# Feed-forward units with a weight scale for each half, and shorter norms at the turn between two layers

## The chip, the cores and the metric

The kernel runs on one core of one Trainium2 chip. The metric is the device time of one execution in microseconds; the median of three runs is compared. Five engines have queues of their own: TensorE (PE; its weight loads are shown as PEld), VectorE (DVE), ScalarE (ACT), GpSimd (POOL) and SyncE (SP), which issues all the DMAs here. They meet in semaphores only.

## What is computed

Three layers in a row, in float32: a retention (attention with a decay mask and no softmax), a mixture of eight experts whose gates are normalised by eight rounds over rows and columns, and a feed-forward layer with a leaky ReLU.

```python
x = retention(q, k, v)                       # 4 x 8 heads x 576 x 64  ->  2304 x 512
# mixture: N, D, E, F = 2304, 512, 8, 1024
for e in range(E):
    out += P[:, e:e+1] * (np.maximum(x @ w1[e], 0.0) @ w2[e])
# feed-forward: 512 -> 2048 -> 512, its weights given in float64
h = x @ w_in
g = np.maximum(0.01 * h, h)
return g @ w_out
```

## The kernel before, in words

**Numbers.** Each float32 operand is scaled by a power of two and split into two float16 parts, high and low; a product is three float16 matmuls. 2 x 2 blocks are multiplied with seven products instead of eight (Winograd's form of Strassen's method), so both operands also need sums of their blocks.

**Units and stages.** The hidden width is worked off in 20 units of 512 columns: 16 of the mixture (two an expert) and 4 of the feed-forward layer (`NU1 = 16`, units 16 to 19). Each unit goes over three thirds of the tokens (`s` = 0 to 2, 384 token pairs each). A stage (unit, s) is 2 x 7 hidden products for the groups g = 0 and 1 (`product_h`, banks hA, hB, hD, hE, line 1028); its second products follow one stage later between the hidden products of the next stage (`group_s`, banks s1a, s1b and s, line 1199). Units 0 and 15 use a plain second product (line 1241). Between both, ScalarE and VectorE split the hidden tiles (hp, hs: lines 1109, 1116, 1119, and sums in lines 1100 to 1146).

**Weights.** `prep_steps(u)` lists the work on a unit's weights as tasks when stage (u - 1, 0) begins. The raw float32 weights come in two halves of 1 MB, part 0 for the first layer and part 1 for the second (`load_raw`, line 186). For each half: four passes of ScalarE that sum magnitudes (`mags`, line 201), a chain of small steps that makes one power of two out of them on all partitions (`scaled`: `total` 207, `quarters` 211 and 213, `beside` 218, `turned` 222 and 223, `spread` 227, `scale` with 159, 160, 165, 250 and 253), four prescaling passes (line 261), and for each group g a `split`: casts on ScalarE (276, 305), differences and block sums on GpSimd (286, 293, 311). In units from 1 on, one chain serves both halves: `scaled(slice(0, 2), maxes(0) + maxes(1))`. The `split` of part 0 asks with `w1_free(g)` that the buffer be free; for g = 1 that is when group 0 of the last stage of the unit before is through. `after(part)` loads the next unit's raw half when a half is split and no operand is on its way to DRAM.

**The order of the work** is written out when the program is built. The class `Order` books each task on engines with estimated costs (`COST`: GpSimd 0.28 us + 0.0020 us an element, and so on) and keeps its own clock `t`. Ahead of and between TensorE's products `tick` calls `pump`, which goes through the queues evac, turn, gate, hid, weights and f64 (hid and weights change places at each call), looks in each at the first 12 tasks (turn: 48) and writes those into their engine's instruction stream whose inputs are done and whose engine is free by the plan within 0.6 us. What isn't out in time is forced: `need((u, "w1", 0))` at the start of stage (u, 0), `need((u, "w2"))` at its first second product. An engine then executes its stream in that order.

**The turn.** While unit 15's second products end, `turn_steps` makes the feed-forward layer's input of each of nine token tiles (two halves h each): sums of magnitudes (lines 1321, 1323), `norms` (a clamp 159, a power of two 160, the factor 1331, the inverse 165), scaling of both halves on GpSimd (1338), four transposes each on TensorE (1348), a copy (64), block sums on GpSimd (532 to 539), casts (64) and low parts (561), and storing to DRAM (486). Stage (16, s) loads what it needs from there (`try_loads`, line 510). `factors` uses the inverses.

Of the kernel before, what the change touches and what calls it, by code (L numbers as in the profile page):

```python
# [8 lines left out]
F32 = mybir.dt.float32  # L9
F16 = mybir.dt.float16  # L10
BF16 = mybir.dt.bfloat16
I32 = mybir.dt.int32
# [3 lines left out]
ALU = mybir.AluOpType  # L16
# [9 lines left out]
NU1 = E * UPE  # L26
# [40 lines left out]
class Order:  # L67


    def __init__(self):  # L70
        self.turn, self.t, self.free = False, 0.0, {e: 0.0 for e in COST}
        self.queues = {q: [] for q in ("evac", "turn", "gate", "hid", "weights", "f64")}

    def book(self, eng, n, after=0.0):
        a, b = COST[eng]
# [20 lines left out]
    def pump(self):  # L96
        self.turn = not self.turn
        qs = list(self.queues.values())
        if self.turn:
            qs[3], qs[4] = qs[4], qs[3]  # L100
        for q in qs:
            for x in q[:WINDOW[q is qs[1]]]:
                if self.ready(x):
                    q.remove(x)
                    self.emit(x)
# [21 lines left out]
def retention_moe_ffn_kernel(ctx: ExitStack, tc: tile.TileContext, qk, vk, wg, wm, wf,  # L127
                             c_dt, c_gq, c_gk, c_id, out):
    nc = tc.nc
    P = 128  # L130
# [39 lines left out]
    wfac = {}  # L170

    raws, raw_at = {}, {}
    turn_last = {}
    order = Order()
    nc_of.update(A=nc.scalar, D=nc.vector, G=nc.gpsimd)

# [11 lines left out]
    def prep_steps(u, small_bank):  # L188
# [16 lines left out]
        def total(p):  # L205
            def f():
                nc.vector.reduce_sum(st["m"][:, p] if u == 0 else m32[:, p], st["mx"][:, p], axis=AX.X)
            return f
# [107 lines left out]
        def add(eng, n, f, deps=(), key=None, cond=None, lat=LAT):  # L316
            x = Task(eng, n, f, deps, (u,) + key, cond, lat)
            tasks.append(x)
            return x
# [6 lines left out]
        def maxes(part, key):  # L326
            there = None if u == 0 else lambda: (u, part) in raws and order.t >= raw_at[u, part] + 8
            return [add("A", 512, mags(part, c), (first_,), key, there) for c in range(4)]

        def scaled(p, mx_, key):  # L330
            t_ = add("D", 10, total(p), mx_, key)
            if u == 0:
                t_ = add("D", 300, top(p), (t_,), key, None, 0.6)
                return add("D", 500, scale(p), (t_,), key, None, 1.2)
            t_ = add("D", 150, quarters, (t_,), key)
            t_ = add("A", 600, beside, (t_,), key)
            t_ = add("D", 150, turned, (t_,), key)
            t_ = add("A", 600, spread, (t_,), key)
            return add("D", 500, scale(p), (t_,), key)

        def scales(part, sc, key):
            return [add("A", 512, prescale(part, c), (sc,), key) for c in range(4)]
# [38 lines left out]
            return tasks  # L381
        ka, kb, k2 = ("w1", 0), ("w1", 1), ("w2",)
        first_ = add(None, 0, begin, (), ka)
        sc = scaled(slice(0, 2), maxes(0, ka) + maxes(1, ka), ka)
        pre0 = scales(0, sc, ka)
        last0 = split(0, 0, pre0[0:2], ka, w1_free(0))
        last0 += split(0, 1, pre0[2:4], kb, w1_free(1))
        after(0, last0, kb)
        pre1 = scales(1, sc, k2)
        last1 = split(1, 0, pre1[0:2], k2, w2_free) + split(1, 1, pre1[2:4], k2, w2_free)  # L390
        after(1, last1, k2)
        return tasks
# [918 lines left out]
    def turn_steps(s, j0):  # L1311

        xs, st = {}, {}

        def sums(j, h):
            def f(e):
                if h == 0:
                    st["l", j] = small.tile([P, 2], F32, tag="l1", name=f"tl1{j}")
                i, o = y[h * NJ + j], st["l", j][:, h:h + 1]
                if e is nc.scalar:  # L1320
                    nc.scalar.activation(junk, i, AF.Abs, accum_out=o)
                else:
                    nc.vector.tensor_reduce(o, i, axis=AX.X, op=ALU.add, apply_absolute_value=True)
            return f

        def norms(j):
            def f():
                s1 = small.tile([P, 2], F32, tag="ts1", name=f"ts1{j}")
                s2 = st["s", j] = small.tile([P, 2], F32, tag="s2", name=f"ts2{j}")
                pow2(s1, st["l", j], f"t{j}")  # L1330
                nc.vector.tensor_scalar(s2, s1, XS, None, op0=ALU.mult)
                recip2(inv.rearrange("p (h j) -> p h j", h=2)[:, :, j], s1)
            return f

        def scaled(j, h):
            def f():
                i = h * NJ + j
                nc.gpsimd.tensor_scalar(y[i], y[i], st["s", j][:, h:h + 1], None, op0=ALU.mult)  # L1338
            return f

        xt = [None, None]

        def turned(j, h):
            def f(e):
                i = h * NJ + j
                ptv = idle_bank(f"xt{i}").rearrange("p (k i) -> p k i", k=NP)
                for k in range(NP):
                    nc.tensor.transpose(ptv[:, k, :], y[i][:, 128 * k:128 * k + 128], ident)
                xt[h] = wtmp.tile([P, NP, P], F32, tag="r64", name=f"tx{i}", bufs=R64)
                copy_on(e, xt[h], ptv)  # L1350
            return f

        j, p, key = j0, turn_last, (1, s)

        def add(eng, n, f, deps, lat=LAT):
            x = Task(eng, n, f, tuple(d for d in deps if d), key, None, lat)
            order.queues["turn"].append(x)
            return x

        y_done = Task(None, 0, None, done=max(order.free["D"], order.free["A"]))  # L1360
        a = [add("AD", 512, sums(j, h), (y_done,)) for h in range(2)]
        a = add("D", 300, norms(j), a)
        b = [add("G", 512, scaled(j, h), (a,)) for h in range(2)]
        t = [add("AD", 512, turned(j, h), (b[h],) + p.get(f"x{h}", ()), 1.5) for h in range(2)]
        operand_tasks(1, j, xt, tuple(t), key, p)
# [11 lines left out]
        try_loads()  # L1377

    def need(key):
        order.flush("weights", lambda k: k == key)  # L1380
        order.wait(max([x.done for x in w_all if x.key == key and x.done], default=None))

# [49 lines left out]
    for n, (u, s) in enumerate(stages):  # L1432
        if s == 0:
            need((u, "w1", 0))
            if u + 1 < NU:
                w_all[:] = w_all[-120:] + prep_steps(u + 1, idle_bank)
                order.queues["weights"] += [x for x in w_all if x.key[0] == u + 1]
            if u == NU1 - 1:
                order.flush("f64", lambda k: True)
        for g in range(2):  # L1440
            if s == 0 and (g == 1 or u == 0):
                need((u, "w1", 1))
            if g == 1 and u == 0:
                logits(s)
                if s == NS - 1:
                    last = ()
                    for f in gate_steps():
                        last = (Task("D", 1500, f, last, "gate", None, 5.0),)
                        order.queues["gate"] += last
            for r in H_ORDER:  # L1450
                need_x(u, s, PROD[r][0])
                product_h(u, s, g, r)
                hpos[0] += 1
                if g == 1:
                    held[0] -= 1
                    try_loads()
                seconds(seconds_by(hpos[0]))
# [70 lines left out]
```

## Time and profile before

| what | us |
| --- | --- |
| median of 3 runs (1801.22 to 1801.67) | 1801.61 |
| the profiled execution | 1801.79 |
| its span | 1799.9 |
| TensorE busy in the span | 1765.2 |
| VectorE busy | 1489.9 |
| ScalarE busy | 1285.3 |
| GpSimd busy | 815.8 |

All rows below are of the profiled execution. A row of a timeline has the start in us from the span's start, the length of a run of equal instructions, engine, line of the kernel, operation, the tile written and the tiles read (buffer and unit numbers left out), shapes, count, and in brackets how long the engine had stood still before it and who released it. Matmuls overlap, so the length of a group is a little more than its step to the next group.

### The profile page before, as it was taken

Reading aid. Unit: us, or ns where it says so; the run is one execution under the profiler, and the core shown is the slowest. Engines: PE = TensorE matmul, PEld = TensorE weight load, DVE = VectorE, ACT = ScalarE, POOL = GpSimd, SP = SyncE. Lnnn points to the kernel's source line nnn. Section 1 sums busy time; section 2 is a strip of 40 time slices with the busy share of each in tenths; the row PEclk is TensorE's granted clock in tenths of the full one; section 3 lists DMA queues with packets and bytes.
Section 4 is the critical chain, followed back from the end, with each engine's and each line's share of the span. In section 5 each row is a group of like instructions: output and inputs, shape, how many; then the busy total and the mean of one; then the engine's idle time right before and its main releaser. Section 6 shows DMA issues by size and latency. Waiting matters only on the chain.

```text
span 1799.9 us, 35885 instructions
## 1 busy us (share of the span) xinstructions
PE 1765.2 (98%) x13686; PEld 1290.1 (72%) x13686; DVE 1489.9 (83%) x2642; ACT 1285.3 (71%) x2808; POOL 815.8 (45%) x782
## 2 busy tenths in 40 slices
PE   9999999999999999999999999999999988999998
PEld 8855677777777777777777777777776555777776
DVE  7955898999888888888898888887776895788886
ACT  6777777777777777777777777777675666877653
POOL 4815362726344463626263444636224972443600
PEclk9999999999999999999999999999999999999999
DMA  9773545446354454454464454443443454444242
GB/s 345 271 252 103 152 127 170 136 150 187 115 171 138 156 156 152 127 170 151 135 190 120 163 147 156 147 143 102 140 150 103 158 170 129 131 125 141 78 128 83
DMA packets 206784, 272.98 MB, mean 152 GB/s; under 512 B 13698, under 2 KB 177556, under 8 KB 201492
## 3 DMA queue, kind: packets, MB, share of 16 engines
q1 hardware_dynamic: 206612, 270.70, 47.9%
q8 instruction: 107, 1.75, 0.4%
q14 instruction: 65, 0.53, 0.1%
HBM read 241.02 MB, written 29.63 MB: 150 GB/s over the span
## 4 chain that ended last, share of the span: by engine, by line
PE 88%; DVE 7%; POOL 2%; issue 1%; ACT 1%; DMA 1%; SPq 0%; DVEq 0%; POOLq 0%; ACTq 0%
PE s L1199 17%; PE hA L1028 12%; PE hB L1028 12%; PE hE L1028 12%; PE s1a L1199 11%; PE s1b L1199 11%; PE hD L1028 6%; PE s L1241 2%; PE s1a L1241 1%; PE s1b L1241 1%; DVE y L1212 1%; DVE xst L561 1%; POOL y L1338 1%; DVE hs L1119 0%; PE xo L721 0%
## 5 line engine op out<-in xcount | busy, mean ns | idle before, releaser
L1028 PEld LDWEIGHTS <-w 128*128 128x128 f16 x5040 | 492.5, 98 | 265.7 <-DMA xring<-x 3.9
L1199 PEld LDWEIGHTS <-hs 128*128 128x128 f16 x3888 | 380.9, 98 | 87.7 <-DVE hs L1119 4.7
L1199 PEld LDWEIGHTS <-hp 128*128 128x128 f16 x2916 | 285.6, 98 | 80.9 <-issue 2.9
L286 POOL TENSOR_TENSOR w<-raw,w 128x384 f16<-128x384 f32 x152 | 163.3, 1088 | 364.1 <-ACT w L276 363.8
L293 POOL TENSOR_TENSOR raw<-raw 128x256 f32<-128x256 f32 x304 | 280.4, 922 | 20.0
L1212 DVE SCALAR_TENSOR_TENSOR y<-s,fac,y 128x256 f32<-128x256 f32 (+1 forms) x322 | 197.6, 614 | 101.2 <-PE s L1199 84.1
L1028 PE MATMUL hE<-xring,w 128*128 128x384 f16 x1440 | 274.7, 326 | 5.3 <-DMA xring<-x 2.1
L1028 PE MATMUL hA<-xring,w 128*128 128x384 f16 x1440 | 276.5, 328 | 2.8 <-ACT w L276 2.3
L1028 PE MATMUL hB<-xring,w 128*128 128x384 f16 x1440 | 274.0, 326 | 0.0
L1199 PE MATMUL s<-w,hs 128*128 128x256 f16 x1932 | 264.2, 273 | 0.8 <-ACT s L1217 0.7
L1119 DVE TENSOR_TENSOR hs<-fs,hs 128x768 f16<-128x768 f32 (+1 forms) x228 | 241.4, 1062 | 8.3 <-ACT hs L1109 6.8
L311 POOL TENSOR_TENSOR w<-raw,w 128x512 f16<-128x512 f32 x148 | 200.4, 1368 | 76.5 <-ACT w L305 76.2
L1109 ACT ACTIVATE hs<-fs 128x768 f16<-128x768 f32 (+1 forms) x228 | 187.6, 823 | 44.4 <-DVE fs L1144 35.1
L446 POOL TENSOR_TENSOR f<-f,e 128x256 f32<-128x256 f32 x64 | 52.8, 825 | 352.5 <-DVE e L438 296.2
L1109 ACT ACTIVATE hp<-fp 128x384 f16<-128x384 f32 x240 | 160.4, 677 | 13.3 <-DVE fp L1067 12.5
L1212 DVE SCALAR_TENSOR_TENSOR y<-s1a,fac,y 128x256 f32<-128x256 f32 (+1 forms) x161 | 98.7, 613 | 50.9 <-ACT s L1217 28.7
L1199 PE MATMUL s1a<-w,hs 128*128 128x256 f16 x972 | 133.4, 273 | 4.6 <-ACT hs L1109 2.4
L1028 PE MATMUL hD<-xring,w 128*128 128x384 f16 x720 | 136.6, 326 | 1.1 <-ACT hD L1056 1.1
L1212 DVE SCALAR_TENSOR_TENSOR y<-s1b,fac,y 128x256 f32<-128x256 f32 (+1 forms) x161 | 98.7, 613 | 43.3 <-ACT s L1217 18.6
L1199 PE MATMUL s1b<-w,hs 128*128 128x256 f16 x960 | 132.1, 273 | 1.8 <-DVE hs L1119 1.4
L1199 PE MATMUL s1a<-w,hp 128*128 128x256 f16 x972 | 132.6, 273 | 1.1 <-DVE y L1212 1.0
L1199 PE MATMUL s1b<-w,hp 128*128 128x256 f16 x960 | 131.6, 274 | 0.5 <-DVE y L1212 0.5
(215 smaller groups left out, 2699.4 us busy)
## 6 DMA issues: line engine op xcount, KB each, us to landing
xring<-x SPq DMA_DIRECT2D x413, 384.0 KB
raw<-in_wm SPq DMA_DIRECT2D x32, 1024.0 KB
r<-in_wf SPq DMA_DIRECT2D x64, 256.0 KB
qk<-in_qk SPq DMA_DIRECT2D x16, 512.0 KB
vk<-in_vk SPq DMA_DIRECT2D x16, 512.0 KB
wf_s<-f SPq DMA_DIRECT2D x32, 256.0 KB
raw<-wf_s SPq DMA_DIRECT2D x8, 1024.0 KB
x<-xst SPq DMA_DIRECT2D x30, 256.0 KB
```

Of the source, the lines that this page charges most:

```text
L286: nc.gpsimd.tensor_tensor(v[0], v[1], v[2], op=ALU.subtract)
L293: nc.gpsimd.tensor_tensor(o, x, y_, op=ALU.subtract)
L311: (nc.gpsimd if u or part else nc.vector).tensor_tensor(lo, r, hi, op=ALU.subtract)
L446: nc.gpsimd.tensor_tensor(dst, dst, cur["tx"].bitcast(F32), op=ALU.mult)
L561: nc.vector.tensor_tensor(st[d][:, :, 1], src[d](), st[d][:, :, 0], op=ALU.subtract)
L1028: nc.tensor.matmul(bank, w[:, a, wi, k, :], x[:, :, b, k, :], start=r in (1, 5) and k == q == 0, stop=k == 1 and q == 2, skip_group_check= ...
L1109: nc.scalar.activation(hid[k][:, 0, a:b], src[:, a:b], AF.Relu if moe and relu else AF.Copy)
L1119: nc.vector.tensor_tensor(t[:, 1, a:b], src[:, a:b], t[:, 0, a:b], op=ALU.subtract)
L1199: nc.tensor.matmul(out_, t[:, a, i, ts], w[:, b, wi, 0, :], start=start and k == 0, stop=k == 5, skip_group_check=True)
L1212: nc.vector.scalar_tensor_tensor(out_, bank, f, out_, op0=ALU.mult, op1=ALU.add)
L1241: nc.tensor.matmul(bank, t[:, a, i, ts], w[:, b], start=l == g == q == 0, stop=l == g == 1 and q == 2, skip_group_check=True)
L1338: nc.gpsimd.tensor_scalar(y[i], y[i], st["s", j][:, h:h + 1], None, op0=ALU.mult)
```

## The change

In units 16 to 19 a half's scale is found from that half alone: part 0 gets its chain after its own four magnitude passes, and part 1's passes and chain are listed behind the splits of part 0. Units 1 to 15 keep one chain for both halves. The six tasks of every such chain go into a queue of their own, which `pump` looks at right behind evac and ahead of the turn, and `need` forces it too. In the turn, the clamp goes (a bound from above on the factor takes its place in the same instruction), the factors of three tiles share one tile, and the inverses of three tiles are computed in one instruction after the third.

```diff
-        self.queues = {q: [] for q in ("evac", "turn", "gate", "hid", "weights", "f64")}
+        self.queues = {q: [] for q in ("evac", "scale", "turn", "gate", "hid", "weights", "f64")}
...
-            for x in q[:WINDOW[q is qs[1]]]:
+            for x in q[:WINDOW[q is qs[2]]]:
...
         def scaled(p, mx_, key):
             t_ = add("D", 10, total(p), mx_, key)
+            first = len(tasks) - 1
...
-            return add("D", 500, scale(p), (t_,), key)
+            t_ = add("D", 500, scale(p), (t_,), key)
+            order.queues["scale"] += tasks[first:]
+            return t_
...
-        sc = scaled(slice(0, 2), maxes(0, ka) + maxes(1, ka), ka)
-        pre0 = scales(0, sc, ka)
+        if u < NU1:
+            sc = [scaled(slice(0, 2), maxes(0, ka) + maxes(1, ka), ka)] * 2
+        else:
+            sc = [scaled(slice(0, 1), maxes(0, ka), ka)]
+        pre0 = scales(0, sc[0], ka)
         last0 = split(0, 0, pre0[0:2], ka, w1_free(0))
         last0 += split(0, 1, pre0[2:4], kb, w1_free(1))
         after(0, last0, kb)
-        pre1 = scales(1, sc, k2)
+        if u >= NU1:
+            sc += [scaled(slice(1, 2), maxes(1, k2), k2)]
+        pre1 = scales(1, sc[1], k2)
...
                 s1 = small.tile([P, 2], F32, tag="ts1", name=f"ts1{j}")
-                s2 = st["s", j] = small.tile([P, 2], F32, tag="s2", name=f"ts2{j}")
-                pow2(s1, st["l", j], f"t{j}")
-                nc.vector.tensor_scalar(s2, s1, XS, None, op0=ALU.mult)
-                recip2(inv.rearrange("p (h j) -> p h j", h=2)[:, :, j], s1)
-            return f
+                s2 = st["s", j] = turn_s[s][:, j - NT_S * s]
+                nc.vector.tensor_scalar(s1.bitcast(I32), st["l", j].bitcast(I32), EXPM, EXPM,
+                                        op0=ALU.bitwise_xor, op1=ALU.bitwise_and)
+                nc.vector.tensor_scalar(s2, s1, XS, XS * 2.0 ** 90, op0=ALU.mult, op1=ALU.min)
+            return f
+
+        def inverses():
+            nc.vector.tensor_scalar(inv_of(s).bitcast(I32), turn_s[s].rearrange("p j h -> p h j").bitcast(I32), -1.0,
+                                    float((254 << 23) + (12 << 23)), op0=ALU.mult, op1=ALU.add)
...
+        if j == NT_S * s + NT_S - 1:
+            order.queues["gate"].append(Task("D", 20, inverses, (a,), "inv"))
...
     def need(key):
+        order.flush("scale", lambda k: k == key)
         order.flush("weights", lambda k: k == key)
```

## Rows read from the trace of the kernel before

**Rows 1.** Busy time by stretches (us; count): PE, PEld, DVE, ACT, POOL; clock; DMA.

```profile
200.00:1350.00 1150.00, 1148.77 (x8777) 858.61 (x8776) 992.68 (x1782) 850.83 (x1859) 514.76 (x497) 1.00 0.48 147
1350.00:1600.00 250.00, 233.77 (x1543) 152.37 (x1542) 189.20 (x327) 176.21 (x387) 135.60 (x125) 0.98 0.42 134
```

**Rows 2.** The same view, finer: the turn, and the stretches of lower clock.

```profile
1410.00:1470.00 60.00, 53.36 (x301) 29.35 (x299) 55.47 (x91) 37.61 (x78) 57.65 (x50) 1.00 0.60 198
...
1470.00:1480.00 10.00, 9.55 (x64) 7.09 (x65) 8.70 (x15) 7.18 (x17) 3.85 (x5) 0.84 0.19 69
...
1510.00:1520.00 10.00, 7.23 (x48) 4.56 (x46) 4.35 (x8) 5.49 (x12) 2.77 (x4) 0.88 0.52 153
1520.00:1530.00 10.00, 6.88 (x37) 3.97 (x36) 4.27 (x4) 5.57 (x12) 8.43 (x10) 0.78 0.00 0
```

**Rows 3.** Timeline of PE where unit 17 begins, and in calm.

```profile
1513.96 0.82 PE L1199 MATMUL s1a<-w,hs 128*128 128x256 f16 x6
1517.05 0.50 PE L1028 MATMUL hA<-xring,w 128*128 128x384 f16 x2 [2.28 <-ACT w L276]
...
1527.93 1.14 PE L1028 MATMUL hB<-xring,w 128*128 128x384 f16 x6
...
1537.63 0.28 PE L1199 MATMUL s1a<-w,hs 128*128 128x256 f16 x1 [0.74 <-DVE hs L1119]
...
1565.50 0.38 PE L1199 MATMUL s1b<-w,hs 128*128 128x256 f16 x2 [0.39 <-POOL w L311]
...
1580.06 0.82 PE L1199 MATMUL s1a<-w,hs 128*128 128x256 f16 x6
...
1584.63 1.14 PE L1028 MATMUL hB<-xring,w 128*128 128x384 f16 x6
```

**Rows 4.** Timeline of ACT, steps of unit 17's weights.

```profile
1446.94 0.63 ACT L201 ACTIVATE junk<-raw 128x512 uint8<-128x512 f32 x1
...
1483.20 0.63 ACT L201 ACTIVATE junk<-raw 128x512 uint8<-128x512 f32 x1
...
1496.47 0.78 ACT L227 COPY m<-t 32x2 f32<-32x2 f32 x4
...
1515.88 0.72 ACT L261 ACTIVATE raw<-raw,sw 128x512 f32<-128x512 f32 x1
```

**Rows 5.** Timeline of POOL: the turn's last tile, then unit 17's first-layer weights.

```profile
1464.37 2.17 POOL L1338 TENSOR_SCALAR y<-y,ts 128x512 f32<-128x512 f32 x1 [0.20 <-DVE inv L165]
...
1476.53 0.77 POOL L532 TENSOR_TENSOR sa<-tx 128x256 f32<-128x256 f32 x1 [6.07 <-DVE tx L64]
...
1517.07 1.78 POOL L286 TENSOR_TENSOR w<-raw,w 128x384 f16<-128x384 f32 x2 [36.77 <-ACT w L276]
1518.93 3.13 POOL L293 TENSOR_TENSOR raw<-raw 128x256 f32<-128x256 f32 x4
1522.78 2.27 POOL L311 TENSOR_TENSOR w<-raw,w 128x512 f16<-128x512 f32 x2 [0.73 <-ACT w L305]
```

**Rows 6.** Timelines of ACT, POOL and PE: unit 16's second half.

```profile
1398.70 0.50 ACT L276 CAST w<-raw 128x384 f16<-128x384 f32 x1
...
1400.19 0.73 ACT L261 ACTIVATE raw<-raw,sw 128x512 f32<-128x512 f32 x1
...
1460.32 2.30 POOL L311 TENSOR_TENSOR w<-raw,w 128x512 f16<-128x512 f32 x2
...
1468.58 0.39 PE L1199 MATMUL s1a<-w,hs 128*128 128x256 f16 x2 [2.15 <-ACT hs L1109]
1470.45 0.40 PE L1199 MATMUL s1a<-w,hs 128*128 128x256 f16 x1 [1.48 <-DVE hs L1119]
```

**Rows 7.** DVE by line: count, ns min/median/max, first and last start in us.

```profile
L159 DVE TENSOR_SCALAR pww<-m x19: 157/162/170, 145.1 to 1654.8; 128x2 f32<-128x2 f32 x19
L159 DVE TENSOR_SCALAR pwt<-tl x9: 155/687/741, 1373.8 to 1462.7; 128x2 f32<-128x2 f32 x9
...
L165 DVE TENSOR_SCALAR inv<-ts x9: 154/159/165, 1374.3 to 1464.1; 128x2 int32<-128x2 int32 x9
```

More of the change, by code (lines that the diff above doesn't have):

```diff
@@ L99, in pump @@
         if self.turn:
-            qs[3], qs[4] = qs[4], qs[3]
+            qs[4], qs[5] = qs[5], qs[4]
         for q in qs:
-            for x in q[:WINDOW[q is qs[1]]]:
+            for x in q[:WINDOW[q is qs[2]]]:
                 if self.ready(x):
@@ L172, in retention_moe_ffn_kernel @@
     raws, raw_at = {}, {}
-    turn_last = {}
+    turn_last, turn_s = {}, {}
     order = Order()
@@ L1358, in add @@
             return x
+        if j == NT_S * s:
+            turn_s[s] = small.tile([P, NT_S, 2], F32, tag="s2", name=f"ts2{s}", bufs=2)
         y_done = Task(None, 0, None, done=max(order.free["D"], order.free["A"]))
@@ L1436, in retention_moe_ffn_kernel @@
                 w_all[:] = w_all[-120:] + prep_steps(u + 1, idle_bank)
-                order.queues["weights"] += [x for x in w_all if x.key[0] == u + 1]
+                order.queues["weights"] += [x for x in w_all if x.key[0] == u + 1 and x not in order.queues["scale"]]
             if u == NU1 - 1:
```

## The prediction

> **What bounds the kernel now.** I read the busy times by stretches first. From 200 to 1350 us TensorE is busy 1148.77 of 1150 us at a granted clock of 1.00; from 1350 to 1600 us it is busy 233.77 of 250 us, at 0.98 [rows 1]. So TensorE bounds the kernel, and an edit on another engine only pays where TensorE stands still or runs at the lower clock. That second stretch is the turn from the first layer to the second: unit 15 ends, its output is normalised, transposed and split into operands, and units 16 and 17 start.
>
> Finer windows [rows 2] show two kinds of trouble in it. From 1410 to 1470 us GpSimd is busy 57.65 and VectorE 55.47 of 60 us: the turn itself. From 1510 to 1530 us TensorE is busy only 7.23 and 6.88 of 10 us with clocks of 0.88 and 0.78, although the turn is over. TensorE's timeline names the reason [rows 3]: at 1517.05 us the first product of unit 17 waits 2.28 us for the first-layer weights of ScalarE's line 276, and the next lines wait on the same tile. The clock falls with the idling.
>
> Why are these weights late? ScalarE's and GpSimd's timelines tell [rows 4, 5]. The sums of magnitudes of unit 17's first half were done by 1447.5 us (the last begins at 1446.94). Those of the second half, whose load waits until unit 16's second layer is split, ended at 1483.7. One scale chain serves both halves, so it starts only then, and crawls behind the hidden tiles: its last four copies begin at 1496.47, the last prescaling pass at 1515.88, when the order written by the planner is out of time and forces it. GpSimd had been idle for 36.77 us when it got its first piece.
>
> **Part 1: own-half scale in units 16 to 19.** Unit 17's chain can start at 1447.5 instead of 1483.7 us. With 68 us until 1515 the four prescalings, four casts and eight GpSimd steps of the first half fit: GpSimd's share is 1.78 + 3.13 + 2.27 = 7.18 us [rows 5]. What the wait cost: from the start of the last group before it (1513.96) to the start of hB (1527.93) is 13.97 us; the same six groups in calm take 1584.63 - 1580.06 = 4.57 us [rows 3]. So 9.40 us, idling and lower clock together, go. A wait of 0.74 us for hidden tiles at 1537.63 [rows 3] comes of it, since VectorE had nothing to do meanwhile; it goes too: **10.14 us**.
>
> Cost: a chain per half instead of one for both adds 8 VectorE steps (a sum, two transposes, two maxima, then three of the scale itself) and 8 ScalarE copies a unit. In units 18 and 19 TensorE has no wait in which these would show, so I set them at nothing; their cover is the slack of the weights, and without it they would cost four times the 2 to 3 us at which part 3 prices such a chain.
>
> One thing moves later. The weights queue looks only at its first 12 tasks. The second group of a first half has exactly 12 (two casts, two differences, four sums, two casts, two differences) and waits until the unit before has finished with its buffer. Before, the second half's magnitude passes stood ahead of these twelve; now they stand behind. In unit 16 one sees the order of before when that gate opened: the cast at 1398.70 and at once the second half's prescaling at 1400.19 [rows 6]. After, at this place four magnitude passes come, then a whole chain, then prescaling. The second-layer weights of unit 16 ended at 1460.32 + 2.30 us before, and TensorE stood until 1470.45 anyway, for hidden tiles (2.15 and 1.48 us) [rows 6]. So a delay of up to 7.8 us is covered by that. I take the delay as 5: the passes take the slots of the prescalings, and GpSimd, full until 1470, started the second layer later than ScalarE offered it.
>
> **Part 2: scale steps served first.** For units 1 to 15 this moves 11 small VectorE steps a unit ahead of the hidden tiles' work. TensorE loses 1.23 us in 1150 there [rows 1], so nothing is to be gained; between -1 and +2 us for a changed order, taken as 0. For units 16 and 17 it is what makes the chain short: 13.3 us from the last magnitude pass to the last copies [rows 4] should become 5 to 9, an estimate from six steps of 0.2 to 0.8 us with a slot of the order between each two.
>
> **Part 3: the norms.** Of four VectorE steps a tile two go (lines 159 and 165), nine times; three joint inversions come instead. In the turn line 159 takes 0.687 us at the median, line 165 0.159 [rows 7]: 0.85 us a tile. Of the six tiles normalised between 1410 and 1470 us that is 5.1 us less of VectorE, in the stretch where it is nearly full. Against it stand the chains that now run in this stretch, unit 16's second half and unit 17's first: 19 steps, at 0.16 to 0.17 us each [rows 7] 3.2 us.
>
> Line 159 says that more is to be counted. With GpSimd idle (the weights' scale, all 19 of them) it takes 0.157 to 0.170 us; in the turn the same form takes up to 0.741 [rows 7]. So two steps of each moved chain that fall beside GpSimd's work can cost 0.53 us more, half of them as I take it: 1.1 us, and the chains 4.3. Net 0.8 us less of VectorE, which I count as 0.8 us of time; bounds are -5.2 (below) and +5.
>
> The Trainium skill (SBUF — State Buffer, section Who interferes with whom) has a rule for this: a VectorE tensor_scalar that uses both ports and a GpSimd instruction exclude each other, whichever issues first holds the ports for its whole length. The trace agrees for line 159, 0.155 against 0.741 us. The rule speaks against the change: it would make most of the moved chains' tensor_scalar steps wait for one GpSimd instruction each. By it the net of part 3 would be near zero or a loss of 1 us.
>
> **The sum.** The profiled execution took 1801.79 us (span 1799.9 and 1.9 around it), 0.2 us above the median of the three runs. 1801.79 - 9.40 - 0.74 - 0.8 = **1790.9 us**. What is late next: in unit 17 its second-layer weights, whose passes start when unit 16's last stage frees the first-layer buffer, near 1500 us. Before, their first use waited 0.39 us for line 311 at 1565.50 [rows 3], so the need comes near 1555; some 38 us of passes, chain and splitting (7.2 of the first half's second group, 17 of its own) leave about 15.
>
> **Rivals.**
> First: the turn's own waits go too. VectorE is behind TensorE's stand at 1468 to 1470 us; 2.15 + 1.48 us of idling and the clock of 0.84 in the ten microseconds after it (1.6 us) make 5.2 us [rows 2, 6]: **1785.7 us**. For it speaks that VectorE is the fuller engine there; against it that GpSimd is as full and the moved chains take most of it back. 0.16.
> Second: unit 17's first half lands in the turn. Its 7.18 us of GpSimd work become ready near 1460, beside tiles 7 and 8. GpSimd has one gap there, the 6.07 us before 1476.53 [rows 5]; what doesn't fall into it, one to three steps of 0.9 to 1.1 us ahead of tile 8's scaling, delays unit 16's third stage, and TensorE pays it with the lower clock on top: 2 to 6 us, **1795 us**. For it: the planner counts 0.28 + 0.002 x 512 = 1.3 us for a scaling that took 2.17 [rows 5], and so sees GpSimd free too early. 0.22, of which 0.03 end within 0.2%.
> Third, slower: unit 16's second half. If the moved chain is as slow in the full turn as unit 17's was, 13.3 us, then with four passes prescaling starts some 20 us late, and the last weights come at 1480 to 1483 in place of 1462.6. TensorE stands 12 us longer, with the lower clock 16: **1807 us**. It decides from a finish near 1478 on, where the loss equals the gain. Against it: the chain is now served ahead of all but evacuations. 0.08.
> Fourth, it doesn't do what it says: unit 17's pieces stay behind the hidden tiles' work, and are forced at 1515 as before: **1801 us**. Against it: 68 us for 16 steps. 0.07.
>
> **How the numbers follow.** The forecast, 1788 to 1794, has 0.47. The range of 1785.0 to 1798.0 takes in most of the first two rivals and leaves out the other two: about 0.8. A run of this kernel can be told from no change by about 0.2%, 3.6 us. Faster: 0.47 + 0.16 + 0.19 = 0.82; the same 0.03 + 0.07 = 0.10; slower 0.08.
>
> **What would show it.** Right: the last prescaling of unit 17's first half begins before 1480 us; no wait of hA on line 276 near 1505; granted clock 1.00 from 1490 to 1530; raw weights of unit 18 loaded 20 us earlier. The norm shows as two short steps a tile. Wrong: s1a waiting on GpSimd's line 311 near 1465 to 1480 (third rival), hA or hE waiting on xring near 1486 (second), or lines 276 and 305 releasing TensorE near 1515 as now (fourth). The order is a plan with its own clock; a stall in the calm stretch, which has none to speak of, would upset the sum too.

## The result and the profile after

The changed kernel takes 1813.51 us (1813.03 to 1817.1, 6 runs), the kernel before 1801.62 us (1800.53 to 1802.86, 6 runs) beside it: 1.007 times as long, 95% interval 1.0057 to 1.0083. It is slower. The profiled execution took 1813.27 us, with a span of 1811.5 us.

Busy time of the changed kernel by stretches, columns as in [rows 1] and [rows 2]:

```profile
200.00:1350.00 1150.00, 1148.15 (x8770) 857.88 (x8768) 1002.24 (x1787) 854.55 (x1864) 510.02 (x498) 1.00 0.48 147
1350.00:1600.00 250.00, 226.28 (x1482) 147.00 (x1481) 180.98 (x311) 168.33 (x374) 132.80 (x120) 0.97 0.43 133
...
1410.00:1470.00 60.00, 54.04 (x306) 30.18 (x304) 53.73 (x96) 42.44 (x96) 55.43 (x50) 1.00 0.58 192
1470.00:1480.00 10.00, 7.00 (x31) 3.80 (x31) 7.27 (x13) 5.78 (x11) 3.06 (x2) 0.66 0.26 96
1510.00:1520.00 10.00, 10.00 (x77) 7.39 (x76) 6.05 (x10) 8.52 (x19) 5.43 (x6) 1.00 0.72 195
1520.00:1530.00 10.00, 10.00 (x79) 7.53 (x78) 5.59 (x9) 8.24 (x21) 2.96 (x2) 1.00 0.44 116
1560.00:1570.00 10.00, 2.35 (x18) 1.56 (x17) 6.70 (x7) 2.71 (x5) 8.52 (x8) 0.83 0.00 0
1570.00:1580.00 10.00, 7.88 (x42) 4.91 (x42) 3.11 (x6) 6.50 (x16) 2.83 (x3) 0.65 0.40 123
```

From 1510 to 1530 us TensorE is now busy throughout at full clock, where [rows 2] had 7.23 and 6.88 us of ten. A hole that was not there stands at 1560 to 1580 us, and the one at 1470 to 1480 us is deeper (7.00 us at 0.66, against 9.55 at 0.84). TensorE's timeline names the releasers; the first two lines answer the last two of [rows 6], those at 1520.56 and 1521.22 us the first two of [rows 3]:

```profile
1471.17 0.61 PE L1207 MATMUL s1a<-w,hs 128*128 128x256 f16 x2 [2.60 <-ACT hs L1117]
1473.05 0.39 PE L1207 MATMUL s1a<-w,hs 128*128 128x256 f16 x1 [1.27 <-DVE hs L1127]
...
1492.87 1.14 PE L1036 MATMUL hA<-xring,w 128*128 128x384 f16 x6 [1.87 <-DMA xring<-x]
...
1520.56 0.82 PE L1207 MATMUL s1a<-w,hs 128*128 128x256 f16 x6
1521.22 1.14 PE L1036 MATMUL hA<-xring,w 128*128 128x384 f16 x6
...
1534.67 0.28 PE L1207 MATMUL s1a<-w,hs 128*128 128x256 f16 x1 [0.60 <-DVE hs L1127]
...
1560.88 0.49 PE L1207 MATMUL s1b<-w,hp 128*128 128x256 f16 x3
1562.76 0.27 PE L1207 MATMUL s1b<-w,hp 128*128 128x256 f16 x1 [1.39 <-ACT w L276]
1565.86 0.38 PE L1207 MATMUL s1b<-w,hp 128*128 128x256 f16 x2 [2.83 <-POOL w L286]
...
1571.26 0.37 PE L1207 MATMUL s1b<-w,hs 128*128 128x256 f16 x1 [4.69 <-ACT w L305]
1572.49 0.59 PE L1207 MATMUL s1b<-w,hs 128*128 128x256 f16 x2 [0.86 <-POOL w L311]
```

Unit 17's first product (1521.22) no longer waits. Its second-layer weights, with 0.39 us of waiting before [rows 3], now hold TensorE for 1.39 + 2.83 + 4.69 + 0.86 = 9.77 us.

To see where time comes and goes, I take the same matmul (the fifth of the six of hD, once in each group) in two timelines and subtract. This table holds its start in the kernel before and the offset of each other kernel, from one profiled execution of each (us; the runs e1 to e16 follow below):

```
product      u16 st1  u16 st2  u16 st3  u17 st1  u17 st2  u17 st2  u19 st3
             group 1  group 1  group 1  group 0  group 0  group 1  group 0
before       1453.31  1484.55  1512.98  1538.40  1566.36  1579.08  1758.69
changed         0.72     4.65     6.60    -2.96     7.79     9.15    11.60
e1_ahead        1.75     4.54     6.75    -1.95    -1.95    -1.95    -1.69
e2_norms       -0.16     0.21     0.16     0.11     0.10     0.10    -0.03
e3_queue        1.01     2.22     3.79     3.07     3.06     3.06     2.57
e4_own          0.10     5.86    14.50    15.27    31.00    31.71    36.50
e10_window     -0.15    -0.81    11.24     1.77     6.35     8.37     8.37
e8_hold         1.38     3.62     3.18    -3.44    10.34    11.95    12.20
e9_nosums       0.89     3.85     5.02    -3.68    -3.68    -3.68    -3.40
e11_both        0.81     2.82     2.14    -4.48     9.29    10.91    11.17
e12_chain       0.97     2.62     4.23    -2.08     5.87     7.55     7.81
e14_slack       0.22    -0.05    -0.53     0.33     0.07     0.07     1.37
e5_ahead17      1.47     3.54     5.76    -2.94    -2.94    -2.94    -2.70
e13_q16         0.35     3.03     5.24    -3.46    -3.46    -3.46    -3.21
e15_q16a17      0.49     3.14     5.36    -3.34    -3.34    -3.34    -3.07
e16_nonorm     -0.69     1.81     4.03    -4.67    -4.67    -4.67    -4.41
```

Where the texts written before the runs speak of the offset of unit 16's third stage or of unit 17's start, they mean where that stage begins: the second and the third column.

The changed kernel gains 6.60 + 2.96 = **9.56 us** at unit 17's start, the predicted 9.40. Against it stand 6.60 - 0.72 = **5.9 us** lost in the turn (third column less the first), 9.15 + 2.96 = **12.1 us** lost at unit 17's second layer, and 11.60 - 9.15 = 2.5 us at the same place in unit 18. (The first column, and the 1 to 2 us that some kernels lose or gain before it, arise mostly in the first 120 us and at one wait near 316 us. e15 and e16, whose work is the same up to the turn, differ by 1.2 us in it, so one offset of that size says little; differences along a row say more.)

ScalarE's and GpSimd's timelines show unit 17's weights, first half then second:

```profile
1447.63 0.63 ACT L201 ACTIVATE junk<-raw 128x512 uint8<-128x512 f32 x1
...
1457.20 0.79 ACT L227 COPY m<-t 32x2 f32<-32x2 f32 x4
...
1484.57 0.71 ACT L261 ACTIVATE raw<-raw,sw 128x512 f32<-128x512 f32 x1
...
1512.33 0.62 ACT L201 ACTIVATE junk<-raw 128x512 uint8<-128x512 f32 x1
...
1529.98 0.62 ACT L201 ACTIVATE junk<-raw 128x512 uint8<-128x512 f32 x1
...
1538.89 0.78 ACT L227 COPY m<-t 32x2 f32<-32x2 f32 x4
...
1546.81 0.72 ACT L261 ACTIVATE raw<-raw,sw 128x512 f32<-128x512 f32 x1
```

```profile
1463.57 2.27 POOL L311 TENSOR_TENSOR w<-raw,w 128x512 f16<-128x512 f32 x2
...
1489.44 4.13 POOL L293 TENSOR_TENSOR raw<-raw 128x256 f32<-128x256 f32 x4
...
1506.63 1.42 POOL L311 TENSOR_TENSOR w<-raw,w 128x512 f16<-128x512 f32 x1 [1.88 <-ACT w L305]
...
1548.98 2.50 POOL L286 TENSOR_TENSOR w<-raw,w 128x384 f16<-128x384 f32 x2 [21.43 <-ACT w L276]
...
1571.29 2.27 POOL L311 TENSOR_TENSOR w<-raw,w 128x512 f16<-128x512 f32 x2 [0.73 <-ACT w L305]
```

The first half's chain starts after 1447.63 us and the weights of its first group are whole at 1508 us, well before 1521. The second half's passes, at 1478.8 to 1483.2 us before [rows 4], run from 1512.33 to 1529.98 us; its last weights end at 1573.56 us, 12.7 us after TensorE comes to the products that want them (1560.88). Before, they ended at 1567.28 us: they are 6.3 us later now and TensorE is there 3.0 us sooner, which is about the 9.4 us of added waiting; with the lower clock behind it, 12.1 us are lost. The same picture as [rows 5], one layer on: GpSimd stands 21.43 us, then gets everything at once. The first line of GpSimd is unit 16's second layer: it ends at 1465.84 us, 3.2 later than before [rows 6].

### The profile page after: what moved, and what is told of

Read it like the earlier page. It is cut to its first block, busy times and chain, and to the rows that moved or that the text cites. A ratio compares the mean times of both kernels' runs of the same rounds, so it can differ in the third digit from the quotient of the medians.

```text
span 1811.5 us, 35925 instructions
## 1 busy us (share of the span) xinstructions
PE 1766.5 (98%) x13686; PEld 1290.8 (71%) x13686; DVE 1496.5 (83%) x2657; ACT 1295.1 (71%) x2840; POOL 811.1 (45%) x782
## 3 DMA queue, kind: packets, MB, share of 16 engines
q8 instruction: 107, 1.75, 0.4%
## 4 chain that ended last, share of the span: by engine, by line
PE 85%; DVE 7%; POOL 4%; DMA 2%; issue 1%; ACT 1%; SPq 0%; DVEq 0%; ACTq 0%; POOLq 0%
PE s L1207 17%; PE hA L1036 12%; PE hB L1036 12%; PE hE L1036 12%; PE s1a L1207 11%; PE s1b L1207 11%; PE hD L1036 6%; PE s L1249 2%; PE s1a L1249 1%; PE s1b L1249 1%; POOL raw L293 1%; DVE y L1220 1%; DVE w L705 1%; POOL y L1350 1%; DVE xt L834 1%
## 5 line engine op out<-in xcount | busy, mean ns | idle before, releaser
L1127 DVE TENSOR_TENSOR hs<-fs,hs 128x768 f16<-128x768 f32 (+1 forms) x228 | 237.3, 1046 | 12.7 <-ACT hs L1117 11.7
L311 POOL TENSOR_TENSOR w<-raw,w 128x512 f16<-128x512 f32 x148 | 193.4, 1321 | 104.1 <-ACT w L305 103.8
```

The source lines that it names most:

```text
L311: (nc.gpsimd if u or part else nc.vector).tensor_tensor(lo, r, hi, op=ALU.subtract)
L1127: nc.vector.tensor_tensor(t[:, 1, a:b], src[:, a:b], t[:, 0, a:b], op=ALU.subtract)
```

## The experiments

Theory A, formed from these rows: the loss is the second half's late passes, and its cure is their place in the list. The rival: the parts themselves (queue, norms, own halves) cost the time.

**e1_ahead**, the changed kernel with the second half's passes listed first:

```diff
         last0 = split(0, 0, pre0[0:2], ka, w1_free(0))
+        if u >= NU1:
+            sc += [scaled(slice(1, 2), maxes(1, k2), k2)]
         last0 += split(0, 1, pre0[2:4], kb, w1_free(1))
         after(0, last0, kb)
-        if u >= NU1:
-            sc += [scaled(slice(1, 2), maxes(1, k2), k2)]
         pre1 = scales(1, sc[1], k2)
```

> The changed kernel, with the magnitude passes and the chain of the second half listed ahead of the second group of the first half, as they stood before. Theory A (the twelve tasks of that group, which wait for their buffer, hide the second half from the queue's window, so its weights come too late): the waits for second-layer weights near 1561 to 1573 us (9.8 us of idling and the lower clock behind it, some 12 us) and near 1655 (2.7 us) go, the gain at the start of unit 17 stays: 1799 +- 3 us; 1794 if the turn's loss of 5 us has the same cause in unit 16. Theory B (ScalarE is too full in unit 16's stages, wherever the passes stand): the second layer stays late, 1808 us or more.

Measured 1799.82 us, ratio 0.9986 (0.9976 to 0.9995). Its waits:

```profile
1472.79 0.61 PE L1207 MATMUL s1a<-w,hs 128*128 128x256 f16 x2 [4.15 <-ACT hs L1117]
1473.78 0.40 PE L1207 MATMUL s1a<-w,hs 128*128 128x256 f16 x1 [0.38 <-DVE hs L1127]
...
1496.70 1.14 PE L1036 MATMUL hB<-xring,w 128*128 128x384 f16 x6 [1.47 <-ACT hB L1046]
...
1563.54 0.38 PE L1207 MATMUL s1b<-w,hs 128*128 128x256 f16 x2 [0.40 <-POOL w L311]
```

The 12.1 and 2.5 us are gone: the second layer waits 0.40 us. The passes end by 1513.1 us and the chain's last copies begin at 1518.37, 20 us sooner. What remains is the turn: 6.75 - 1.75 = 5.0 us. The two waits for hs last 4.53 us together where they lasted 3.63 before [rows 6], only 0.9 us more; but the granted clock behind them is 0.66 instead of 0.84:

```profile
1470.00:1480.00 10.00, 6.83 (x30) 4.31 (x31) 7.26 (x12) 4.84 (x9) 2.32 (x2) 0.66 0.33 125
```

**e2_norms, e3_queue, e4_own**, the kernel before with one part of the change each: the turn's norms, the scale queue, the own halves.

```diff
 e2  norms(j), inverses(), turn_s as in the change
 e3  queue "scale" as in the change
 e4  if u < NU1 / if u >= NU1 in prep_steps as in the change
```

> The kernel before with the shorter norms alone. Theory A (the norms help the turn a little, and its loss of 5 us in the changed kernel comes from the moved weights): 1797 to 1801 us, the waits near 1517 us as before. Theory C (the shorter norms cost the turn its 5 us, by the shared factor tile or by another order of VectorE and GpSimd): 1806 us.

Measured 1803.31 us, ratio 1.0001 (0.9992 to 1.0011): the norms are worth nothing, and cost nothing in the turn (offset 0.16 at unit 17's start).

> The kernel before with the queue for the scale steps alone; the scale still waits for both halves. Theory A: unit 17's chain shrinks from 17 us to some 8, its prescaling begins near 1493 us and not 1503, and most of the 9.4 us at 1517 go, nothing moves into the turn: 1792 to 1796 us. Theory D (serving the chain ahead of the turn's and the hidden tiles' work costs them more than it gives): 1802 us or more.

Measured 1803.46 us, ratio 1.0003 (0.9993 to 1.0013). The queue alone shortens the chain from 13.3 to 11.2 us only (1485.43 to 1496.64) and does not bring unit 17's first layer in time: its passes are still at 1481 to 1485 us, its prescaling at 1503, and the gain at unit 17's start is 3.79 - 3.07 = 0.7 us. With it 2.8 us are lost in the turn (1.01 to 3.79). In the third stage TensorE waits 1.93 us for hs at 1503.28, where it waited 0.60 us before. The 1.2 us of the second stage come without more waiting: hs is waited for 2.17 and 1.49 us as before, but the granted clock from 1470 to 1480 us is 0.66 instead of 0.84. Why it stays low for longer there is not shown.

> The kernel before with the own-half scale alone; chains are served in the weights queue. Theory A: unit 17's first layer is in time, its second layer as late as in the changed kernel or later, because the chain is slower: 1813 to 1820 us. Theory D (the queue is what costs): 1800 us or less.

Measured 1839.44 us, ratio 1.0205 (1.019 to 1.022).

```profile
1474.01 0.37 PE L1204 MATMUL s1a<-w,hs 128*128 128x256 f16 x1 [6.81 <-ACT w L305]
...
1474.04 2.27 POOL L311 TENSOR_TENSOR w<-raw,w 128x512 f16<-128x512 f32 x2 [4.39 <-ACT w L305]
```

Without the queue, unit 16's own second half is late: its weights end at 1476.3 us. That is the prediction's third rival, and the queue is what keeps it away from unit 16. The time is 19 us above the upper end of Theory A, which names unit 17 alone. The offset grows by 14.4 us in unit 16, with a wait of 7.48 us for xring at 1499.68 that follows, and by 16 more in unit 17.

**e10_window**, the changed kernel with the look-ahead of 24 tasks instead of 12:

```diff
-LAT, SLACK, WINDOW = 0.15, 0.6, (12, 48)
+LAT, SLACK, WINDOW = 0.15, 0.6, (24, 48)
```

> The changed kernel with the look-ahead of all queues but the turn's widened from 12 to 24 tasks, nothing else. Theory A, the twelve waiting tasks of a first half's second group hide the second half's passes: the passes of unit 17's second half begin well before 1512 us (1475 to 1495), the wait of 9.8 us at 1562 to 1573 us goes, time 1797 to 1803 us. Theory B, the order of the list delays them in another way: the waits stay, 1811 to 1815 us. As the window is that of the hidden tiles' queue too, some us of change elsewhere are possible.

Measured 1810.08 us, ratio 1.0043 (1.0029 to 1.0057).

```profile
1495.40 2.08 PE L1036 MATMUL hA<-xring,w 128*128 128x384 f16 x6 [9.86 <-DMA xring<-x]
...
1566.11 6.00 POOL L311 TENSOR_TENSOR w<-raw,w 128x512 f16<-128x512 f32 x4
...
1571.05 0.58 PE L1207 MATMUL s1b<-w,hs 128*128 128x256 f16 x2 [3.24 <-POOL w L311]
```

The time lies between the two theories. The loss at the second layer halves (8.37 - 1.77 = 6.6 us), but mostly because TensorE comes there 4.7 us later (1.77 against -2.96): the last weights end at 1572.11 us, 1.5 us sooner than in the changed kernel. Only the first of the four passes moves, to 1470.35 us; the others still come at 1511 to 1530, among the second group's casts. And the wider view reorders the turn itself: TensorE waits 9.86 us for xring. So the window of 12 is at most a small part of the cause. What decides is the order of the list, which e1 changes by itself. In e1, too, three of the four passes begin only at 1510.23 to 1512.47 us, but they stand together; in the changed kernel, with the second group's pieces ahead of them, three begin at 1525.60 to 1529.98. What holds them back there, task by task, is not shown.

**e8_hold**, e1 with the prescaling of unit 17's first half held until unit 16's second stage is done:

```diff
+            held_ = (lambda: (NU1, 1, 1) in h_done) if (u, part) == (NU1 + 1, 0) else None
-            return [add("A", 512, prescale(part, c), (sc,), key) for c in range(4)]
+            return [add("A", 512, prescale(part, c), (sc,), key, held_) for c in range(4)]
```

> The kernel of e1_ahead, but the prescaling of unit 17's first half may not start before the hidden products of unit 16's second stage are done (near 1487 us). In e1_ahead two of these passes ran on ScalarE at 1465.16 and 1466.92 us, the cast of tile 7's sa went to VectorE (0.83 us) and hp was late; s1a then waited 4.15 us for hs at 1472.79, against 2.15 us in the kernel before. Theory A, the prescaling in the turn costs this part: that wait goes back to 2 to 2.5 us, the offset of unit 16's third stage against the kernel before falls from 4.5 to about 2.2 us, and the time from 1799.8 to about 1797.5 us. Theory B, it comes from something else (the turn's own order after 16 us of shift): wait above 3.5 us, time 1799 to 1801 us. Theory C, the later pieces then collide with the hidden tiles after 1490: the gain is given back there, 1799 us, and unit 17's first product waits on lines 276 or 311.

Measured 1814.81 us, ratio 1.0072 (1.0059 to 1.0085). In the turn the hold does give most of the loss back: 3.18 - 1.38 = 1.8 us in place of 5.0, none of it in the third stage (3.62 to 3.18). But not as expected: the waits for hs stay (4.14 and 0.39 us, as in e1).

```profile
1472.42 0.60 PE L1208 MATMUL s1a<-w,hs 128*128 128x256 f16 x2 [4.14 <-ACT hs L1118]
...
1573.81 0.37 PE L1208 MATMUL s1b<-w,hs 128*128 128x256 f16 x1 [4.17 <-ACT w L305]
```

And the held pieces push the second half's passes to 1521.5 to 1528 us, so the first layer's second group (3.0 us) and the second layer are late: 11.95 + 3.44 = 15.4 us. **e11_both** is e8 with the scale steps served first only from unit 16 on:

```diff
+            if u >= NU1:
                 order.queues["scale"] += tasks[first:]
```

> The kernel of e8_hold, with the scale steps served first only from unit 16 on (units 1 to 15 keep them in the weights' queue). e3_queue lost 0.9 us at 316 us to one wait of hB for line 1049 and kept it. Theory A, that wait comes of the scale steps put ahead of the hidden tiles: it goes, and the time is 0.9 us below e8_hold's (1796.6 us if that is 1797.5). Theory B, it is chance of the order: equal to e8_hold within 0.5 us.

Measured 1814.93 us: its profiled span is 1.1 us below e8's and the offset before the turn 0.6 us smaller, with no difference between the medians.

**e9_nosums**, e1 without GpSimd's eight differences of line 293 in unit 17's first half:

```diff
+                if (u, part) == (NU1 + 1, 0):
+                    return
                 b11, b21, b22, b12 = (blocks(part, g)[0][:, i] for i in range(4))
```

> The kernel of e1_ahead, with the eight GpSimd differences between blocks (line 293) of unit 17's first half left out; unit 17's weights are wrong by that, the plan's own clock still books them. In e1_ahead four of them run at 1489.32 to 1493.64 us, and VectorE's steps beside them take 1.08 us (lines 1152 and 1154, 128x384) and 2.35 us (line 1127, two) against 0.55 and 1.89 us in the kernel before, where GpSimd stands idle then; hB waits 1.47 us at 1496.70. Theory A, GpSimd's pieces stretch VectorE's hidden-tile steps: the steps return to 0.55 and 1.9 us, that wait goes, the offset of the third stage's second group falls from 6.75 to about 4.5 us, time about 1797.5 us. Theory B, the order on ScalarE makes the wait: no change, 1799.8 us.

Measured 1798.01 us, ratio 0.9974 (0.9963 to 0.9985). VectorE's timeline in e1, where GpSimd runs line 293 from 1489.32 to 1493.64 us:

```profile
1489.97 1.08 DVE L1152 TENSOR_TENSOR fs<-fs,fp 128x384 f32<-128x384 f32 x1
1490.97 1.08 DVE L1154 TENSOR_TENSOR fs<-fp,fs 128x384 f32<-128x384 f32 x1
1491.97 1.07 DVE L1108 TENSOR_TENSOR fs<-fp,fs 128x384 f32<-128x384 f32 x1
1492.97 2.35 DVE L1127 TENSOR_TENSOR hs<-fs,hs 128x768 f16<-128x768 f32 x2
```

and the same four steps in e9 (its line numbers are two higher), where GpSimd stands idle from 1488.55 to 1504.04 us:

```profile
1489.29 0.54 DVE L1154 TENSOR_TENSOR fs<-fs,fp 128x384 f32<-128x384 f32 x1
1489.76 0.55 DVE L1156 TENSOR_TENSOR fs<-fp,fs 128x384 f32<-128x384 f32 x1
1490.23 0.54 DVE L1110 TENSOR_TENSOR fs<-fp,fs 128x384 f32<-128x384 f32 x1
1490.74 1.90 DVE L1129 TENSOR_TENSOR hs<-fs,hs 128x768 f16<-128x768 f32 x2
```

Half the time: that is GpSimd's share, and hB's wait of 1.47 us goes. A wait of 0.84 us on hs takes its place, so the third stage's loss falls by 1.0 us only, from 2.2 (4.54 to 6.75) to 1.2 (3.85 to 5.02). The rest of the 1.8 us is the start of the kernel.

**e12_chain**, e1 with unit 17's first chain held until the first group of unit 16's second stage is done:

```diff
+            late = (lambda: (NU1, 1, 0) in h_done) if (u, p.stop) == (NU1 + 1, 1) else None
-            t_ = add("D", 10, total(p), mx_, key)
+            t_ = add("D", 10, total(p), mx_, key, late)
```

> The kernel of e1_ahead, but the scale chain of unit 17's first half may not start before the first group of unit 16's second stage is done (near 1467 us); the prescaling follows it, so both are out of the stretch in which tile 7 is normalised. In e8_hold, where the prescaling alone was held, the chain's VectorE steps at 1451.9, 1453.3, 1457.2 and 1459.4 us stood between the turn's, tile 7's norm came at 1454.84 instead of 1453.45 us, GpSimd took the sums of sb first and both scalings at a stretch, and hs stayed 4.1 us late. Theory A, the chain's steps in the turn make hs late: the wait for hs near 1470 us falls to 2.2 and 1.5 us as in the kernel before, the offset of unit 16's third stage against it from 4.5 to about 2.2 us, time about 1797.5 us. Theory B, the plan's order there shifts for any cause (the norms and the queue are enough): the wait stays at 4 us, time 1799 to 1800 us.

Measured 1809.46 us, ratio 1.0043 (1.003 to 1.0055): unit 17's second group and second layer are late again. In the turn, the loss over unit 16's second stage falls from 4.54 - 1.75 = 2.8 to 1.65 us, with 3.20 + 0.73 us of waiting for hs. So holding the chain, and all that follows it, takes off some 1.1 us of it, not all.

**e14_slack**, a control: the kernel before with SLACK 0.65 instead of 0.6.

> A control: the kernel before with one constant of its plan changed (a step may be issued when its engine is free within 0.65 instead of 0.6 us), no part of the change. Theory A, the order in the turn follows small shifts of the plan's clock: the offset of unit 17's start against the kernel before is 1 us or more in either direction, and the time moves with it, 1799 to 1806 us. Theory B, the order is stable: within 0.5 us there, 1801.5 to 1803 us in all.

Measured 1802.98 us, ratio 1.0004 (0.9995 to 1.0013). The waits in the turn change their places (2.65 us on POOL's y at 1468.90, none on ACT's hs), the sum hardly does: from 0.22 to -0.53 us over the turn. One such shift can't exclude that a turn that loses 5 us is in part chance of the order, but it speaks against it.

**e5_ahead17, e13_q16, e15_q16a17, e16_nonorm**, reliefs of e1: unit 16 with one chain for both halves (e5); the scale steps first only from unit 16 on, the edit of e11 (e13); both (e15); both without the new norms (e16).

```diff
 e5, e15, e16
-        if u < NU1:
+        if u <= NU1:
...
-        if u >= NU1:
+        if u > NU1:
```

> The kernel of e1_ahead, but unit 16 keeps one chain for both halves as in the kernel before; units 17 to 19 have a chain of their own for each half. Theory A, unit 16's second chain at 1408 to 1414 us and its later second layer cost part of the turn: the offset at unit 16's second stage falls from 2.2 to about 1 us, and the time to about 1798.5 us. Theory B, all of the turn's loss is unit 17's first half (and the order): 1799 to 1800.5 us.

> The kernel of e1_ahead, with the scale steps served first only from unit 16 on. Theory A, the 0.9 us at 316 us go and nothing else changes: 1798.9 us. Theory B, the order in units 1 to 15 is worth nothing by itself: 1799.8 us. If the turn's order is as sensitive as e3_queue and e8_hold suggest, the offset across the turn (4.3 us in e1_ahead from unit 16's second stage to unit 17's start) differs by 1 to 2 us although nothing there is changed.

> The kernel of e1_ahead with both reliefs that showed a gain by themselves: the scale steps served first only from unit 16 on, and unit 16 with one chain for both halves. Theory A, they add up (0.8 us for unit 16's chain, 1.2 us for the order in units 1 to 15): 1797.8 us, with an offset at unit 17's start of about 4.5 us against the kernel before. Theory B, the first part of the turn's loss is unit 17's chain and the norms alone and these two only moved the start of the turn: the wait for hs stays at 4.1 us, time 1798 to 1799 us.

> The kernel of e15_q16a17 with the turn's norms of the kernel before (four VectorE steps a tile, no joint inversion). Theory A, the norms are worth nothing in the turn, as e2_norms showed them by themselves: time within 0.7 us of e15_q16a17's, the wait for hs near 1470 us about 4 us. Theory B, their earlier end and the inversion at the stage's end make hs late: the wait falls below 3 us and the time by 1 to 2 us. Theory C, they do save what was counted for them (0.8 us): the time rises by about that.

| kernel | us | ratio (95%) | lost in the turn |
| --- | --- | --- | --- |
| e5_ahead17 | 1799.06 | 0.9983 (0.9974 to 0.9992) | 4.3 |
| e13_q16 | 1798.57 | 0.998 (0.9971 to 0.9989) | 4.9 |
| e15_q16a17 | 1798.30 | 0.998 (0.9971 to 0.9989) | 4.9 |
| e16_nonorm | 1797.51 | 0.9974 (0.9964 to 0.9985) | 4.7 |

The last column is the third of the table of offsets less the first. The wait for hs stays above 4.1 us in all four. e13 saves the 0.9 us at 316 us; unit 16's chain is worth 0.7 us alone (e5) and nothing on top (e15). e16's 0.8 us under e15 stand in its offset before the turn, where the two kernels do not differ, so the norms are again worth nothing in it. e16 is the fastest kernel of the study; its interval and e15's overlap.

## Why the prediction was wrong, by its steps

**Part 1, the wait removed: right.** 9.40 us were to go at unit 17's start; 9.56 went, and the clock is 1.00 from 1510 to 1530 us. The last prescaling began at 1484.57 us, not before 1480 as foreseen, and was early enough. The wait of 0.74 us was to go with it and did not: 0.60 us stand at 1534.67. The reason given, VectorE without work meanwhile, was not its cause.

**"What is late next": the step that failed.** It named the right thing, unit 17's second-layer weights, and gave it 38 us of work from 1500 us, leaving "about 15". Measured: first pass at 1512.33, last weights at 1573.56, 61 us, against a need at 1560.88. The start was taken 12 us too early; 6.6 of these are the offset that unit 16's last stage had by then, and by which the need moved too. Of the 38 us, 14 were left for passes and chain; with the prescaling they took 35 (to 1547.5), the passes alone 18, because the second group's casts and the hidden tiles stand between them. This spread is what e1 takes away: three of its passes begin as late, but all end by 1513.1. The splitting took 25 from GpSimd's first piece instead of 17, with waits for ScalarE's casts in it. A margin of 15 us out of an untimed chain of 38 should have had a rival of its own, with the price of the wait removed: 9.8 us of waiting, with clocks of 0.83 and 0.65 from 1560 to 1580 us, made 12.1.

**The twelve tasks.** The prediction saw that the second half's passes now stand behind the second group and worked out the delay in unit 16, where 5 us were expected and 3.2 came. TensorE did not wait for these weights, as said; but on GpSimd the scaling of tile 8 follows them, and ends at 1473.06 us instead of 1470.46. The prediction did not work the delay out in unit 17, where the same order has no wait to hide in. e1 shows the order of the list to be the cause; e10 shows that a wider window does not cure it.

**Third rival.** Its mechanism, a moved chain too slow for the second layer, is what made the kernel slower (0.08 was given to it), at a price of the same order (16 us foreseen, 12.1 + 2.5 measured). It named unit 16, and e4 shows it there without the queue; with the queue it struck one unit later.

**Part 2 and the second rival.** The queue was taken as 0. e3 prices it: 1.0 us in units 1 to 15, of which 0.9 come at one wait for line 1049 near 316 us, and 2.8 us in the turn. Unit 17's chain takes 9.6 us in the changed kernel (1447.63 to 1457.20), a little more than the 5 to 9 foreseen. The second rival's 2 to 6 us for unit 17's first half in the turn came, 5.9 us, with 0.22 given, and so did its sign: hA waits 1.87 us for xring at 1492.87. But no GpSimd step of unit 17 stood ahead of tile 8's scaling: all of those run after 1486 us, when the scalings are done. What did stand ahead is unit 16's line 311, 3.2 us later than before; that this made xring late is not shown. With e1's order xring is waited for 0.25 us only; there the loss is hs, the clock behind it, and hB. e8 removes 3.2 of these 5.0 us by holding the prescaling and all behind it, e12 1.7 by holding the chain, e9 0.9 by leaving out line 293. Why the waits for hs last 4.53 us even with the prescaling held (e8) stays open: VectorE does a cast that ScalarE did before, and gets to hp's difference later, but no run isolates this.

**Part 3, the norms: mis-sized.** VectorE's busy time from 1410 to 1470 us falls from 55.47 to 53.73 us, more than the 0.8 counted. It moves the end by nothing (e2: 0.9992 to 1.0011; e16 likewise). An engine that is 90% busy beside others as full is not thereby the one that ends last. The surcharge of 0.53 us for a step of the scale beside GpSimd did not come either. It was read from steps of two columns [rows 7], and a chain of one half has steps of one: the four single-column steps of unit 17's chain, at 1459.40 to 1459.84 us, take 0.14 to 0.15 us while GpSimd is at line 293, and a two-column step (line 1338) a microsecond earlier takes 0.69 (the next, line 1340, begins at 1459.32 between two steps of GpSimd and takes 0.17). VectorE, then GpSimd, in the changed kernel:

```profile
1458.60 0.69 DVE L1338 TENSOR_SCALAR ts<-tl 128x2 int32<-128x2 int32 x1
...
1459.40 0.15 DVE L159 TENSOR_SCALAR pww<-m 128x1 f32<-128x1 f32 x1
```

```profile
1457.22 2.85 POOL L293 TENSOR_TENSOR raw<-raw 128x256 f32<-128x256 f32 x3
```

The fourth rival is out: the pieces were not forced. The range of 1785 to 1798 us missed 1813.5. Even e1, without the late second half, stays above it at 1799.82: the turn's 5 us, of which the sum knew nothing outside the second rival, are a second term that failed.

## What to carry to other kernels

When a wait is removed by starting one chain sooner, time the next chain on the same engines by its last need, step by step, in every unit it concerns: here the gain of 9.6 us was real, and a second half whose passes came 34 us later cost 12.1. Pieces that ran while the bounding engine stood still were free; beside its work they cost a part of what they saved: the turn lost 4 to 5 us in e1 and its reliefs, of which holding these pieces took off 3.2 (e8). And where a planner serves lists in order, the order of the list is as much a part of an edit as the work it adds: swapping two lines (e1) was worth 14 us.

## What the runs showed of the hardware

VectorE's two-input steps of 128x384 take 0.54 to 0.55 us with GpSimd idle and 1.07 to 1.08 us beside GpSimd's line 293, in the same place of two kernels (e1, e9). The Trainium skill (SBUF — State Buffer, section Who interferes with whom) says that a VectorE instruction with two SBUF inputs contends with a GpSimd instruction that reads SBUF; the trace agrees. The prediction looked at that section for the scale's tiny steps only, and not for the hidden tiles beside which the moved GpSimd work would fall.
